# Attention, Fourier mixing and feed-forward in one kernel: the first batch without transfers inside SBUF, and a first feed-forward whose two layers follow one another

## The chip, the cores and the metric

The kernel runs on one core of a Trainium2 chip. A core has five engines with queues of their own: TensorE (PE in the profile, with its weight loads as PEld), VectorE (DVE), ScalarE (ACT), GpSimd (POOL) and SyncE (SP, which here only issues DMAs). Each engine takes its instructions in the order of the program, and semaphores tie the engines together. The metric is the device time of one execution in microseconds (us); the profile is of one execution.

## What is computed

The reference takes q, k and v of 8 batches, 8 heads, 576 positions and 64 columns, and two weight matrices (512 x 2048 and 2048 x 512). Cut to what matters:

```python
scores = scale * np.matmul(q, k.transpose(0, 1, 3, 2))
scores = np.where(block_i >= block_j, scores, -1e9)       # blocks of 64 positions
attn = softmax(scores)                                    # over the last axis
x = np.matmul(attn, v), heads side by side                # (8, 576, 512)
u = x + real(fft(fft(x, axis=1), axis=2))
un = (u - mean(u)) / sqrt(var(u) + 1e-6)                  # over the last axis
out = u + np.maximum(un @ w_ch1, 0) @ w_ch2
```

## The kernel before, in words

**Order of the work.** A planner written into the kernel (`Step`, `Queue`, `issue`, and the loop at L922) decides in which order steps are emitted. Each step has a cost on PE, a chain of costs on other engines, keys it comes after, and a place. There are seven lanes: loads of heads, their preparation, v, the maxima, scores, values, and the transform; besides them a lane of weight steps (`weight_lane`) that fills gaps, and the feed-forward as a filler of PE (`feed_steps`). Steps of batch 1 and later are taken only when the last weight step is emitted (key "w32", L930). PE keeps the order of emission (`mm`, `tp`, L193 to L198); the other engines' order follows from a simulation of the program when it is built.

**Precision.** Numbers of 32 bits are split in a high part that a matmul takes exactly and a rest. For a head, `lead` (L292) writes the high part of q and k into the tile `LEAD` (64 rows of data, below them 8 rows that make the mask, and one row, `KS - 1`, that holds for each query a shift: minus its largest score). `rest` (L304) writes the remainders into the tile `REST`: of q by DVE in its upper 64 rows, of k by POOL in its lower 64 rows. `lead_copies` (L299) fills the other halves of `REST` with the high parts, by two DMAs from SBUF to SBUF, so that one matmul of 128 rows gives both mixed products. There are three buffers of each.

**Attention of a head.** `max_part` (L371) computes scores in the high parts alone and reduces them on DVE to a maximum for each query, in the tile `M` (L388 to L394). `shift` (L398) transposes the five columns of `M` on PE, negates them on ACT (L403, tile `mt`) and sends them by a DMA to the last row of `LEAD` (L405). In batch 0 `quick` (L295) puts these DMAs on ACT's queue, later on SP's. `scores` (L417) then needs two matmuls for each piece of columns: `rest` by `rest` (L430) and `lead` by `lead` (L432), the latter with mask and shift. ACT takes the exponential twice, to fp16 (`ph`, L434) and to fp32 (`p`, L435), and POOL subtracts (`pl`, L436). `values` (L441) multiplies by v, whose parts `VH` and `VL` come from L339 and L340; DVE divides by the sums (L471 to L474), and after every second head SP stores x to DRAM (L479).

**Transform.** `fourier_steps` (L522) loads and gathers the batch, folds it (L549 to L564, tiles `tmp`, `fs`), multiplies by cosines and sines (tiles `zc`, `zs`, `ZT`) and adds to u. `normalized_steps` (L678) normalizes a half of a batch, transposes it (L703) and hands it to `feed_steps` with a running number; number 1 is the first half of batch 0.

**Weights.** They are loaded as 18 blocks (`LANDS`, L811): 14 of two row groups that land in parts of the tile `W` not yet used, four single ones in tiles `u`. `weight_single` (L830) merges the two words of each number on DVE (L836 to L838) and sums squares on ACT (L839); `weight_loads` (L821) then lets SP load ahead, up to `FLIGHT` blocks counted from the one at hand. `weight_scale` (L844) finds a scale, `weight_parts` (L859) makes the two fp16 parts: for w1 on ACT and POOL (L863, L866, L867), for w2 on ACT and DVE (L863, L869).

**Feed-forward.** `first` (L729) computes a column block f of the hidden layer in `h` (twelve matmuls); for every second f ACT and DVE make its two fp16 parts `gh` and `gl` (L749, L750), in tiles with two buffers each. `second` (L752) multiplies them by w2 into `acc`. The order is: first layer of f = 0, 1, then always the first layer of the next two and the second layer of the last two (L785 to L793). In feed number 1 a first-layer step comes after the parts of w1 that it reads, a second-layer step after its part of w2.

Of the kernel before, what the change touches and what calls it, by code (L numbers as in the profile page):

```python
# [22 lines left out]
P = 128  # L23
# [15 lines left out]
FLIGHT = 3  # L39
# [6 lines left out]
KS = KM + 1  # L46
# [25 lines left out]
def _constants():  # L72
# [45 lines left out]
    masks = np.zeros((9, 64 + 2 * S))  # L118
    masks[8, 64 + S:] = 1.0
# [59 lines left out]
def tile_attn_fourier_ffn(  # L179
# [45 lines left out]
    REST = [const.tile([P, 2 * S], F32R, name=f"rest{i}") for i in range(NB)]  # L225
    M = [const.tile([P, 6], F32, name=f"M_{i}") for i in range(2)]
    DEN = [const.tile([P, 5], F32, name=f"DEN_{i}") for i in range(2)]
# [67 lines left out]
    def quick(h):  # L295

        return nc.scalar if h < H else nc.sync

    def lead_copies(h):  # L299
        x0, x1 = REST[h % NB].bitcast(F32), LEAD[h % NB].bitcast(F32)  # L300
        quick(h).dma_start(x0[D:P, 0:S], x1[0:D, 64:64 + S])
        quick(h).dma_start(x0[0:D, S:], x1[0:D, 64 + S:])

    def rest(h, which):  # L304
# [4 lines left out]
        else:  # L309
            nc.gpsimd.tensor_tensor(x0[D:P, S:], raw[:, S:], x1[0:D, 64 + S:], op=ALU.subtract)  # L310
# [38 lines left out]
    def prepare_lane():  # L349
        for h in range(B * H):  # L350
# [4 lines left out]
            yield Step(lambda: lead_copies(h), 0.0, ("A1.0" if h < H else "Q1.2", "L2.2"), (("T", h),), ("TC", h), place=h - 0.9)  # L355
# [15 lines left out]
    def max_part(h, n):  # L371

        m = M[h % 2]
# [13 lines left out]
        if n == 0:  # L387
            nc.vector.tensor_reduce(  # L388
                m[:, 0:6:5], t[:, 0:128].rearrange("p (x y) -> p x y", y=64), axis=AX.X, op=ALU.max
            )  # L390
        j, lo, hi = parts[-1]
        nc.vector.tensor_reduce(m[:, j:j + 1], t[:, at - hi:at], axis=AX.X, op=ALU.max)  # L392
        if n == 3:
            nc.vector.tensor_tensor(m[:, 4:5], m[:, 4:5], m[:, 5:6], op=ALU.max)  # L394
# [3 lines left out]
    def shift(h):  # L398
# [5 lines left out]
        dst = LEAD[h % NB][KM:KS, 0:640].rearrange("r (j p) -> r j p", j=5)  # L404
        quick(h).dma_start(dst.bitcast(F32), mt.bitcast(F32))  # L405
# [11 lines left out]
    def scores(h, n):  # L417
# [9 lines left out]
        for c, lo, width in chunks:  # L427
            first, last = P * c + lo, P * c + lo + width
            keys = S + (P * c if c < 4 else S - P)
            mm(t[:, w:w + width], x0[:, keys:keys + P], x0[:, first:last], start=(w == 0), stop=False, skip_group_check=True)  # L430
# [53 lines left out]
    def score_lane():  # L484
        for h in range(B * H):
            for n, (i, at, chunks) in enumerate(PIECES):
                w = sum(x[2] for x in chunks)
                yield Step(
                    lambda n=n: scores(h, n), w / 1200.0, (_a(w), _a(w), "B", _g(w)),
                    (("X", h), ("TC", h), ("T2", h, 0), ("T2", h, 1)), ("S", h, i) if n else None, True,  # L490
# [3 lines left out]
    def max_lane():  # L494
        for h in range(B * H):
# [5 lines left out]
            yield Step(lambda: shift(h), 0.12, ("A0.26", "B", "A0.5" if h < H else "Q0.6", "L2.2"), (("M", h),), ("X", h), True, place=h - 0.6)  # L501
# [222 lines left out]

# [288 lines left out]
```

## Time and profile before

| what | value |
| --- | --- |
| median of 3 runs | 1315.72 us (1313.14 to 1316.76) |
| the profiled execution's own time | 1315.5 us |
| its span, first to last instruction | 1313.7 us |
| PE busy | 1184.2 us, 90% of the span |
| DVE, ACT, POOL busy | 671.9, 548.5, 530.0 us |
| moved by DMA | 99.10 MB, mean 75 GB/s |

Busy times are sums over the span, so an engine with a small share can still be what a stage waits for. In the rows that follow, a group of instructions has line, engine, operation, output <- input, and count; a row in order of time begins with its start and its length in us, and what stands in brackets is how long the engine was idle before it and what ended that. Names ending in q (ACTq, SPq) are the instructions by which an engine issues DMAs.

### The profile page before, as it was taken

To read this page: it belongs to the slowest core of one execution; us is meant where nothing else is said; L and a number is where in the kernel's file an instruction comes from. 1 tells how busy PE (TensorE), PEld (TensorE's weight loads), DVE (VectorE), ACT (ScalarE), POOL (GpSimd) and SP (SyncE) were. 2 spreads that over 40 slices of the span, in tenths; PEclk is the share of its full clock that TensorE was granted. 3 is DMA by queue.
4 is the path that set the end of the run, shared out by engine and by line. 5 is a ranking of instruction groups with operands and counts; after the bars stand their busy time and mean duration, and the time that the engine had idled before them with its cause. 6 is when DMAs were issued, how large, how long until landed. Compare 5 with 4: busy or idle time off the path is not lost.

```text
span 1313.7 us, 25264 instructions
## 1 busy us (share of the span) xinstructions
PE 1184.2 (90%) x10068; PEld 886.7 (67%) x10068; DVE 671.9 (51%) x1440; ACT 548.5 (42%) x1137; POOL 530.0 (40%) x578
## 2 busy tenths in 40 slices
PE   3464469999898999999999999999899999999998
PEld 2363357777676777677777777777677767767665
DVE  6983776445645564655546544746372432412211
ACT  3569355545354444444545354544543112111110
POOL 4668143444544553455443645436442500300000
PEclk9955679999699999999999999999999999999999
DMA  9756213232223223322242133223211000000000
GB/s 280 230 175 177 93 29 77 84 106 64 61 65 92 76 50 90 93 76 51 80 115 75 44 96 104 73 70 86 79 30 49 30 12 17 22 1 17 16 17 17
DMA packets 55941, 99.10 MB, mean 75 GB/s; under 512 B 7709, under 2 KB 26605, under 8 KB 55696
## 3 DMA queue, kind: packets, MB, share of 16 engines
q1 hardware_dynamic: 52176, 87.56, 23.5%
q0 software_dynamic: 2288, 7.54, 1.9%
q10 hardware_dynamic: 1360, 2.38, 0.6%
q8 instruction: 80, 1.31, 0.4%
q14 instruction: 37, 0.30, 0.1%
HBM read 58.46 MB, written 18.87 MB: 59 GB/s over the span
## 4 chain that ended last, share of the span: by engine, by line
PE 76%; DVE 10%; ACT 4%; DMA 3%; POOL 3%; issue 3%; SPq 0%; ACTq 0%; DVEq 0%; POOLq 0%
PE h L194 27%; PE acc L194 26%; PE ps L194 16%; PE av L194 5%; POOL pl L436 2%; PE ps L197 1%; DVE M L392 1%; DVE W L837 1%; DMA W<-in_moe_w_ch_dram 1%; DVE rest L308 1%; DVE W L838 1%; ACT lead L293 1%; DVE tmp L549 1%; DMA U<-xd,rows 1%; DVE W L836 1%
## 5 line engine op out<-in xcount | busy, mean ns | idle before, releaser
L194 PE MATMUL h<-uh,W 128*128 128x256 f16 x2304 | 434.9, 275 | 0.0
L436 POOL TENSOR_TENSOR pl<-p,ph 128x288 f16<-128x288 f32 (+1 forms) x256 | 257.9, 1017 | 395.8 <-ACT p L435 249.6
L194 PEld LDWEIGHTS <-W 128*128 128x128 f16 x3456 | 325.8, 99 | 64.3 <-issue 4.0
L194 PE MATMUL acc<-W,gh 128*128 128x512 f16 x1152 | 347.2, 383 | 0.0
L194 PE MATMUL h<-ul,W 128*128 128x256 f16 x1152 | 316.2, 274 | 0.0
L194 PE MATMUL acc<-W,gl 128*128 128x512 f16 x576 | 220.1, 382 | 0.4 <-DVE gl L750 0.4
L750 DVE SCALAR_TENSOR_TENSOR gl<-h,gh 128x512 f16<-128x512 f32 x144 | 98.9, 687 | 227.3 <-ACT gh L749 227.2
L194 PE MATMUL ps<-lead 72*128 72x64 f32 (+9 forms) x700 | 196.5, 342 | 12.5 <-ACT lead L293 6.8
L749 ACT ACTIVATE gh<-h 128x512 f16<-128x512 f32 x144 | 85.9, 596 | 268.4 <-PE h L194 267.7
L434 ACT ACTIVATE ph<-ps 128x512 f16<-128x512 f32 (+1 forms) x229 | 116.0, 507 | 121.0 <-PE ps L194 119.7
L194 PEld LDWEIGHTS <-gh 128*128 128x128 f16 x1152 | 101.0, 99 | 87.8 <-issue 8.2
L392 DVE TENSOR_REDUCE M<-ps 128x1 f32<-128x320 f32 (+3 forms) x235 | 120.5, 527 | 47.9 <-PE ps L194 46.7
L194 PE MATMUL av<-VH,pl 128*128 128x65 f16 x960 | 115.9, 200 | 31.7 <-POOL pl L436 31.5
L194 PEld LDWEIGHTS ps<-lead 72*128 72x128 f32 (+1 forms) x700 | 125.6, 201 | 20.8 <-ACT lead L293 6.8
L194 PEld LDWEIGHTS <-ph 128*128 128x128 f16 x1920 | 113.0, 103 | 34.1 <-DVE x L474 8.4
L310 POOL TENSOR_TENSOR rest<-raw,lead 64x576 fp32r<-64x576 f32 x64 | 116.2, 1816 | 23.3 <-ACT lead L293 18.5
L194 PE MATMUL av<-VH,ph 128*128 128x65 f16 x960 | 118.1, 202 | 8.2 <-DVE x L474 7.6
L194 PE MATMUL ps<-rest 128*128 128x64 f32 (+2 forms) x345 | 121.6, 360 | 1.8 <-DVE M L392 1.1
L435 ACT ACTIVATE p<-ps 128x512 f32<-128x512 f32 (+1 forms) x229 | 115.9, 506 | 10.2 <-POOL pl L436 10.1
L194 PE MATMUL av<-VL,ph 128*128 128x64 f16 x960 | 117.3, 200 | 0.0
L194 PEld LDWEIGHTS <-pl 128*128 128x128 f16 x960 | 93.6, 102 | 34.9 <-POOL pl L436 34.8
L308 DVE TENSOR_TENSOR rest<-raw,lead 64x576 fp32r<-64x576 f32 x64 | 60.0, 938 | 88.4 <-ACT lead L293 88.3
(171 smaller groups left out, 1376.7 us busy)
## 6 DMA issues: line engine op xcount, KB each, us to landing
raw<-in_qk_dram SPq DMA_DIRECT2D x64, 288.0 KB
rest<-lead SPq DMA_DIRECT2D x112, 144.0 KB
W<-in_moe_w_ch_dram SPq DMA_DIRECT2D x14, 1024.0 KB
V<-in_v_dram SPq DMA_DIRECT2D x32, 320.0 KB
xd<-x SPq DMA_DIRECT2D x32, 256.0 KB
out_dram<-u SPq DMA_DIRECT2D x32, 256.0 KB
u<-xd SPq DMA_DIRECT2D x8, 512.0 KB
dft<-in_c_dft_dram POOLq DMA_DIRECT2D x1, 2606.0 KB, 11.3
```

The costliest lines, as they stand in the source:

```text
L194: return tc.keep_in_program_order(nc.tensor.matmul(*args, **kw))
L197: return tc.keep_in_program_order(nc.tensor.transpose(*args, **kw))
L293: nc.scalar.copy(LEAD[h % NB][0:D, 64:], raws[h])
L308: nc.vector.tensor_tensor(x0[0:D, 0:S], raw[:, 0:S], x1[0:D, 64:64 + S], op=ALU.subtract)
L310: nc.gpsimd.tensor_tensor(x0[D:P, S:], raw[:, S:], x1[0:D, 64 + S:], op=ALU.subtract)
L392: nc.vector.tensor_reduce(m[:, j:j + 1], t[:, at - hi:at], axis=AX.X, op=ALU.max)
L434: nc.scalar.activation(ph[:, at:at + w], t[:, 0:w], AF.Exp, scale=0.125)
L435: nc.scalar.activation(p32[:, 0:w], t[:, 0:w], AF.Exp, scale=0.125)
L436: nc.gpsimd.tensor_tensor(pl[:, at:at + w], p32[:, 0:w], ph[:, at:at + w], op=ALU.subtract)
L549: nc.vector.tensor_tensor(e[0:r], X[c][0:r], U[c][0:r], op=op)
L749: nc.scalar.activation(gh, t, AF.Relu)
L750: nc.vector.scalar_tensor_tensor(gl, t, 0.0, gh, op0=ALU.max, op1=ALU.subtract)
```

## The change

It has four parts. (1) For the heads of batch 0 (h < H) nothing is copied inside SBUF. `lead_copies` is not called; `scores` makes the mixed products by two matmuls of 64 rows, one with the high part of k and the rest of q, one the other way round, and POOL writes the rest of k into the upper 64 rows. The shift row is made by PE: the maxima are written into a column of a tile of zeros, `MZ`, so that a matmul of 97 columns (`shift_row`) puts them, transposed, at partition 96 of PSUM, from where ACT writes the row of `LEAD` directly. For that the row moves from partition 72 to 96 (`KS = D + 33`), with rows of zeros between; the loaded mask has 33 rows in place of 9. `shift_row` is two steps, of four matmuls and of one. `MZ` lies in the memory of the transform's tiles `zc0` and `zc1` and is cleared at the start. (2) Later heads use the same row, and their DMAs stay on SP. (3) `FLIGHT` is 2 in place of 3. (4) Feed number 1 does its first layer for all 16 blocks and then its second; the tiles `gh` and `gl` from f = 5 on lie in the transform's tiles `zc`, `zs` and `fs`.

```diff
--- before.py
+++ after.py
@@ -36,14 +36,14 @@
 AHEAD = (1.5, 6.0)
 FREE = 0.5
 
-FLIGHT = 3
+FLIGHT = 2
 
 PSHIFT = 5
 
 BANKS = {"ps": 3, "h": 2, "acc": 2}
 
 KM = D + 8
-KS = KM + 1
+KS = D + 33
 
 
 def _a(width):
@@ -115,8 +115,8 @@
         [chunks(csh, csl), chunks(ssh, ssl), stack_c, stack_s, chunks(cdh, cdl), chunks(sdh, sdl), tail], 1
     ).astype(np.float32)
 
-    masks = np.zeros((9, 64 + 2 * S))
-    masks[8, 64 + S:] = 1.0
+    masks = np.zeros((KS - D, 64 + 2 * S))
+    masks[-1, 64 + S:] = 1.0
     for c in range(4):
         masks[c, 64 + 128 * c:128 + 128 * c] = 1.0
         masks[c, 64 + S + 128 * c + 64:64 + S + 128 * c + 128] = NEG
@@ -223,7 +223,22 @@
     NB = 3
     LEAD = [const.tile([KS, 64 + 2 * S], F32R, name=f"lead{i}") for i in range(NB)]
     REST = [const.tile([P, 2 * S], F32R, name=f"rest{i}") for i in range(NB)]
+
     M = [const.tile([P, 6], F32, name=f"M_{i}") for i in range(2)]
+    MZ = [
+        work.tile([P, 2, NCOS], F32R, name=f"zc{i}", bufs=1).bitcast(F32).rearrange("p x n -> p (x n)") for i in range(2)
+    ]
+    for i in range(2):
+        nc.vector.memset(MZ[i], 0.0)
+
+    def maximum(h, j):
+        at = j if h >= H else KS * (j + 1) - 1 if j < 5 else KS * 5 + 1
+        return (M if h >= H else MZ)[h % 2][:, at:at + 1]
+
+    def outer_maxima(h):
+
+        return M[h % 2][:, 0:6:5] if h >= H else MZ[h % 2][:, KS - 1:KS * 5 + 2:KS * 4 + 2]
+
     DEN = [const.tile([P, 5], F32, name=f"DEN_{i}") for i in range(2)]
     VH = [const.tile([P, 5, 2, D + 1], F16, name=f"VH_{i}") for i in range(2)]
     VL = [const.tile([P, 5, 2, D], F16, name=f"VL_{i}") for i in range(2)]
@@ -292,14 +307,10 @@
     def lead(h):
         nc.scalar.copy(LEAD[h % NB][0:D, 64:], raws[h])
 
-    def quick(h):
-
-        return nc.scalar if h < H else nc.sync
-
     def lead_copies(h):
         x0, x1 = REST[h % NB].bitcast(F32), LEAD[h % NB].bitcast(F32)
-        quick(h).dma_start(x0[D:P, 0:S], x1[0:D, 64:64 + S])
-        quick(h).dma_start(x0[0:D, S:], x1[0:D, 64 + S:])
+        nc.sync.dma_start(x0[D:P, 0:S], x1[0:D, 64:64 + S])
+        nc.sync.dma_start(x0[0:D, S:], x1[0:D, 64 + S:])
 
     def rest(h, which):
 
@@ -307,7 +318,8 @@
         if which == 0:
             nc.vector.tensor_tensor(x0[0:D, 0:S], raw[:, 0:S], x1[0:D, 64:64 + S], op=ALU.subtract)
         else:
-            nc.gpsimd.tensor_tensor(x0[D:P, S:], raw[:, S:], x1[0:D, 64 + S:], op=ALU.subtract)
+            at = slice(0, D) if h < H else slice(D, P)
+            nc.gpsimd.tensor_tensor(x0[at, S:], raw[:, S:], x1[0:D, 64 + S:], op=ALU.subtract)
 
     def load_v(g):
         V = vraw[g] = work.tile([P, 5, 2, D], F32, name="V", bufs=1)
@@ -352,7 +364,8 @@
                 lambda: lead(h), 0.0, ("A1.15",), (("L", h),), ("T", h), place=h - 1.0,
                 need=(("S", h - NB, 2),) if h >= NB else (),
             )
-            yield Step(lambda: lead_copies(h), 0.0, ("A1.0" if h < H else "Q1.2", "L2.2"), (("T", h),), ("TC", h), place=h - 0.9)
+            if h >= H:
+                yield Step(lambda: lead_copies(h), 0.0, ("Q1.2", "L2.2"), (("T", h),), ("TC", h), place=h - 0.9)
             yield Step(lambda: rest(h, 0), 0.0, (_d(S),), (("T", h),), ("T2", h, 0), place=h - 0.8)
             yield Step(lambda: rest(h, 1), 0.0, (_g(S),), (("T", h),), ("T2", h, 1), place=h - 0.8)
 
@@ -370,7 +383,6 @@
 
     def max_part(h, n):
 
-        m = M[h % 2]
         x = LEAD[h % NB][0:KM]
         kh = x[:, 64 + S:]
         qh = lambda j: x[:, P * j:P * (j + 1)]
@@ -386,12 +398,12 @@
             at += hi - lo
         if n == 0:
             nc.vector.tensor_reduce(
-                m[:, 0:6:5], t[:, 0:128].rearrange("p (x y) -> p x y", y=64), axis=AX.X, op=ALU.max
+                outer_maxima(h), t[:, 0:128].rearrange("p (x y) -> p x y", y=64), axis=AX.X, op=ALU.max
             )
         j, lo, hi = parts[-1]
-        nc.vector.tensor_reduce(m[:, j:j + 1], t[:, at - hi:at], axis=AX.X, op=ALU.max)
+        nc.vector.tensor_reduce(maximum(h, j), t[:, at - hi:at], axis=AX.X, op=ALU.max)
         if n == 3:
-            nc.vector.tensor_tensor(m[:, 4:5], m[:, 4:5], m[:, 5:6], op=ALU.max)
+            nc.vector.tensor_scalar(maximum(h, 4), maximum(h, 4), maximum(h, 5), None, op0=ALU.max)
 
     MAXPARTS = (((0, 0, 64), (4, 512, 576), (1, 0, 192)), ((2, 0, 320),), ((3, 0, 448),), ((4, 0, 512),))
 
@@ -401,8 +413,23 @@
         tp(t[0:5, 0:P], M[h % 2][:, 0:5], ident)
         mt = work.tile([5, P], F32R, name="mt", bufs=2)
         nc.scalar.activation(mt, t[0:5, 0:P], AF.Copy, bias=float(8.0 * PSHIFT * np.log(2.0)), scale=-1.0)
-        dst = LEAD[h % NB][KM:KS, 0:640].rearrange("r (j p) -> r j p", j=5)
-        quick(h).dma_start(dst.bitcast(F32), mt.bitcast(F32))
+        dst = LEAD[h % NB][KS - 1:KS, 0:640].rearrange("r (j p) -> r j p", j=5)
+        nc.sync.dma_start(dst.bitcast(F32), mt.bitcast(F32))
+
+    def shift_row(h, part):
+
+        t = ps_tile()
+        js = range(4) if part == 0 else range(4, 5)
+        for j in js:
+            at = P * (j - js[0])
+            mm(
+                t[0:KS, at:at + P], MZ[h % 2][:, KS * j:KS * (j + 1)], ident, start=(j == js[0]), stop=(j == js[-1]),
+                skip_group_check=True,
+            )
+        nc.scalar.activation(
+            LEAD[h % NB][KS - 1:KS, P * js[0]:P * (js[-1] + 1)], t[KS - 1:KS, 0:P * len(js)], AF.Copy,
+            bias=float(8.0 * PSHIFT * np.log(2.0)), scale=-1.0,
+        )
 
     probs = {}
 
@@ -427,7 +454,15 @@
         for c, lo, width in chunks:
             first, last = P * c + lo, P * c + lo + width
             keys = S + (P * c if c < 4 else S - P)
-            mm(t[:, w:w + width], x0[:, keys:keys + P], x0[:, first:last], start=(w == 0), stop=False, skip_group_check=True)
+            if h < H:
+                k1, q1 = x1[0:D, 64 + keys:64 + keys + P], x1[0:D, 64 + first:64 + last]
+                mm(t[:, w:w + width], k1, x0[0:D, first:last], start=(w == 0), stop=False, skip_group_check=True)
+                mm(t[:, w:w + width], x0[0:D, keys:keys + P], q1, start=False, stop=False, skip_group_check=True)
+            else:
+                mm(
+                    t[:, w:w + width], x0[:, keys:keys + P], x0[:, first:last], start=(w == 0), stop=False,
+                    skip_group_check=True,
+                )
             keys, w = keys + 64, w + width
             mm(t[:, w - width:w], x1[:, keys:keys + P], x1[:, 64 + first:64 + last], start=False, stop=True, skip_group_check=True)
         p32 = work.tile([P, 512], F32, name="p32", bufs=2)
@@ -486,8 +521,8 @@
             for n, (i, at, chunks) in enumerate(PIECES):
                 w = sum(x[2] for x in chunks)
                 yield Step(
-                    lambda n=n: scores(h, n), w / 1200.0, (_a(w), _a(w), "B", _g(w)),
-                    (("X", h), ("TC", h), ("T2", h, 0), ("T2", h, 1)), ("S", h, i) if n else None, True,
+                    lambda n=n: scores(h, n), w / (800.0 if h < H else 1200.0), (_a(w), _a(w), "B", _g(w)),
+                    (("X", h), ("T2", h, 0), ("T2", h, 1)) + ((("TC", h),) if h >= H else ()), ("S", h, i) if n else None, True,
                     need=(("V", h - 1, 2 * i),) if h else (), place=h,
                 )
 
@@ -498,7 +533,13 @@
                     lambda n=n: max_part(h, n), 0.03 + sum(x[2] - x[1] for x in MAXPARTS[n]) / 2400.0, (f"D{(0.65, 0.49, 0.63, 0.93)[n]}",),
                     (("T", h),), ("M", h) if n == 3 else None, True, place=h - 0.6,
                 )
-            yield Step(lambda: shift(h), 0.12, ("A0.26", "B", "A0.5" if h < H else "Q0.6", "L2.2"), (("M", h),), ("X", h), True, place=h - 0.6)
+            if h < H:
+                yield Step(lambda: shift_row(h, 0), 1.0, (_a(4 * P),), (("M", h),), ("X0", h), True, place=h - 0.6)
+                yield Step(lambda: shift_row(h, 1), 0.3, (_a(P),), (("M", h),), ("X", h), True, place=h - 0.6)
+            else:
+                yield Step(
+                    lambda: shift(h), 0.12, ("A0.26", "B", "Q0.6", "L2.2"), (("M", h),), ("X", h), True, place=h - 0.6
+                )
 
     def value_lane():
         for h in range(B * H):
@@ -722,6 +763,9 @@
     n_norm = 0
     feeds = []
 
+    KEEP = [(f"z{x}{m}", [P, 2, n], 1) for x, n in (("c", NCOS), ("s", NSIN)) for m in range(2)]
+    KEEP += [(f"fs{m}", [P, 2, KCOL], 1) for m in range(2)]
+
     def feed_steps(me, uh, ul, us, stores):
         acc = []
         gs = {}
@@ -742,8 +786,14 @@
                 i += 1
             if f % 2 == 0 or part < NK - 1:
                 return
-            gh = work.tile([P, 4 * P], F16, name="gh", bufs=2)
-            gl = work.tile([P, 4 * P], F16, name="gl", bufs=2)
+            if me == 1 and f > 3:
+
+                name, shape, bufs = KEEP[f // 2 - 2]
+                both = work.tile(shape, F32R, name=name, bufs=bufs).rearrange("p x n -> p (x n)").bitcast(F16)
+                gh, gl = both[:, 0:4 * P], both[:, 4 * P:8 * P]
+            else:
+                gh = work.tile([P, 4 * P], F16, name="gh", bufs=2)
+                gl = work.tile([P, 4 * P], F16, name="gl", bufs=2)
             for x in range(2):
                 gs[f - 1 + x] = (gh[:, 2 * P * x:2 * P * (x + 1)], gl[:, 2 * P * x:2 * P * (x + 1)])
             nc.scalar.activation(gh, t, AF.Relu)
@@ -782,6 +832,11 @@
                     ("F", me) if f == NF - 1 and n == 1 else None,
                 )
 
+        if me == 1:
+            for steps in (first_steps, second_steps):
+                for f in range(NF):
+                    yield from steps(f)
+            return
         yield from first_steps(0)
         yield from first_steps(1)
         for f in range(0, NF, 2):
```

## The prediction

> **What bounds the kernel now.** I read the page's slices first: TensorE (PE) is full for most of the span and thin at its beginning. So I cut the span where the work changes and read busy times by stretch (columns: stretch, its length, then busy us and instructions of PE, PEld, DVE, ACT, POOL, the granted clock, DMA share, GB/s).
>
> ```profile
> 0.00:27.00 27.00, 6.66 (x22) 5.40 (x23) 16.46 (x40) 7.70 (x10) 8.85 (x26) 1.00 0.92 277
> 27.00:62.00 35.00, 16.37 (x117) 13.80 (x116) 34.97 (x47) 20.17 (x43) 22.26 (x12) 1.00 0.79 252
> 62.00:103.00 41.00, 27.96 (x288) 25.02 (x287) 34.42 (x67) 29.26 (x61) 29.81 (x23) 0.67 0.59 190
> 103.00:127.00 24.00, 11.31 (x110) 9.38 (x109) 8.91 (x20) 21.47 (x41) 21.79 (x20) 0.50 0.56 147
> 127.00:180.00 53.00, 24.75 (x157) 20.31 (x157) 36.35 (x87) 21.57 (x49) 20.00 (x26) 0.63 0.25 81
> 180.00:210.00 30.00, 25.81 (x213) 18.79 (x213) 23.50 (x42) 23.19 (x44) 13.29 (x11) 0.86 0.20 52
> 210.00:320.00 110.00, 108.30 (x992) 81.86 (x991) 54.67 (x129) 52.50 (x114) 44.27 (x43) 0.98 0.29 79
> 320.00:360.00 40.00, 33.76 (x244) 25.84 (x243) 26.37 (x60) 15.08 (x31) 22.46 (x31) 0.74 0.27 74
> ```
>
> After 210 PE is nearly full, apart from a dip at 320 to 360. The change touches no work there, so it gains what it brings forward before 210. Batch 0's attention ends at 127; then a chain of latencies (store of x, gather, transform, normalization) runs to 180, where feed-forward begins. In 27 to 62 VectorE (DVE) is the bound: 34.97 of 35 us. In 103 to 127 it is idle and ACT and POOL are 90% busy: heads that came late meet the scaling of w1 (L863, L866, L867).
>
> Why are the heads late? Head 0, on PE, ACT, DVE and POOL in order of time:
>
> ```profile
> 15.01 0.58 PE L194 MATMUL h<-rest 128*128 128x288 f32 x1 [0.53 <-DMA rest<-lead]
> 25.35 0.61 PE L194 MATMUL h<-lead 73*128 73x288 f32 x1 [9.77 <-DMA lead<-mt]
> ...
> 12.74 0.27 ACT L403 ACTIVATE mt<-acc 5x128 fp32r<-5x128 f32 x1 [2.52 <-PE acc L197]
> 19.57 1.27 ACTq L405 DMA_DIRECT2D lead<-mt  x1
> 20.88 0.83 ACT L339 ACTIVATE VH<-V,vacc 128x640 f16<-128x640 f32 x1 [7.88 <-issue]
> ...
> 6.76 0.75 DVE L308 TENSOR_TENSOR rest<-raw,lead 64x576 fp32r<-64x576 f32 x1 [4.55 <-ACT lead L293]
> 10.93 1.34 DVE L394 TENSOR_TENSOR M<-M 128x1 f32<-128x1 f32 x1
> 21.75 0.88 DVE L340 SCALAR_TENSOR_TENSOR VL<-V,vacc,VH 128x640 f16<-128x640 f32 x1 [4.43 <-ACT VH L339]
> ...
> 25.50 8.35 POOL L310 TENSOR_TENSOR rest<-raw,lead 64x576 fp32r<-64x576 f32 x1 [13.24 <-ACT lead L293]
> ```
>
> The maxima are complete at 12.27, the row is ready at 13.0, its DMA is issued only at 19.57, and PE goes on at 25.35. ACT stands behind that issue for 7.88 us, DVE behind ACT for 4.43, POOL has nothing for 13.24. This is what the change takes away.
>
> **The change part by part.** *Transfers of batch 0.* Gone are, for eight heads, two copies and one row, all issued by ACT:
>
> ```profile
> L301 ACTq DMA_DIRECT2D rest<-lead x8: 468/492/561, 7.1 to 92.7; - x8
> L302 ACTq DMA_DIRECT2D rest<-lead x8: 468/608/615, 7.7 to 93.3; - x8
> L405 ACTq DMA_DIRECT2D lead<-mt x8: 728/736/1271, 19.6 to 104.3; - x8
> ...
> 87.20 0.63 ACT L434 ACTIVATE ph<-acc 128x512 f16<-128x512 f32 x1
> ```
>
> That is 8 x (0.49 + 0.61 + 0.74) = 14.7 us of ACT's queue. Added is a 512-wide copy from PSUM per head, like the 0.63 us row, and a 128-wide one in place of L403: 8 x 0.6 = 5 us. ACT is about 10 us lighter. The new copies wait for PE as L403 did, with the same exponentials and weight squares queued behind them.
>
> PE gets dearer. The scores' first matmul becomes two of 64 rows, so the columns of the `rest` matmuls run once more; five fp32 matmuls of 128 columns replace one transpose. The nearest rows:
>
> ```profile
> 26.24 0.57 PE L194 MATMUL ps<-rest 128*128 128x448 f32 x1
> 26.61 0.57 PE L194 MATMUL ps<-lead 73*128 73x448 f32 x1
> ...
> 172.08 1.08 PE h L197 x4
> ...
> 97.01 0.30 PE L194 MATMUL h<-vacc,ones 128*128 128x1 f32 x2
> ```
>
> At half clock 448 columns take 0.37 us from start to start, so the 1600 columns of a head take 1.3. Four transposes of 128 fp32 columns last 1.08, or (1.08 - 0.42) / 3 = 0.22 each, their single duration being 0.42:
>
> ```profile
> L197 PE MATMUL h<-ident,un x8: 421/421/456, 172.1 to 174.5; 128*128 128x128 f32 x8
> ```
>
> One fp32 matmul that is no transpose (L330) left two records, so a shift matmul costs 0.22 to 0.44, the five 1.1 to 2.2. Together 2.4 to 3.5 us per head at half clock, 19 to 28 for eight; PE is idle 65 of the first 127 us, so I put it at nothing on the path and keep the price for a rival. The Trainium skill, FP8 and Floating Point Precision, section TensorE Precision Notes, says that true fp32 takes four passes through the array. By that, at the cold 1.2 GHz of TensorE: Matmul & The Clock Gate, the five would be an estimate of 5 x 128 x 4 / 1.2 GHz = 2.1 us; the two records here fit the dearer end, and the sum would stay.
>
> From the maxima to a head's scores the new path is 2 to 3.5 us (those matmuls, 0.6 and 0.3 of ACT); for head 0 it was 13.1. What passes to the end of batch 0? At least DVE's gap, 4.4 us, because DVE bounds the next stretch. At most all idle time of DVE after its start at 6.8: 127 - 94.8 busy - 6.8 = 25 us. Between them I look at the pitch of heads once the weights let go:
>
> ```profile
> 78.35 0.21 DVE L471 TENSOR_SCALAR DEN<-av,vacc 128x5 f32<-128x5 f32 x1
> 102.35 0.22 DVE L471 TENSOR_SCALAR DEN<-av,vacc 128x5 f32<-128x5 f32 x1 [0.82 <-PE av L194]
> 125.62 0.23 DVE L471 TENSOR_SCALAR DEN<-av,vacc 128x5 f32<-128x5 f32 x1 [2.00 <-PE av L194]
> ```
>
> Three heads in 24.0 us: 8.0 each. If heads stand one further when the weights end, 4.4 + 8.0 = 12.4 us go. I take **10**, near the 9.77 that PE waited for that first row.
>
> *Two weight blocks ahead in place of three* (the loop asks up to its own number plus FLIGHT).
>
> ```profile
> L836 DVE TENSOR_SCALAR W<-W x14: 674/688/1893, 12.3 to 84.3; 128x1024 int32<-128x1024 int32 x14
> ...
> 78.39 0.37 SPq L826 DMA_DIRECT2D W<-in_moe_w_ch_dram  x1
> 129.84 9.13 SPq L826 DMA_DIRECT2D u<-in_moe_w_ch_dram  x4
> ```
>
> A block is merged every 5.5 us, and the last of the 14 came 5.9 us after its issue. A block asked for one step later on SP may come late by up to that pitch; on the other side the third raw head shares the DMA with fewer weights at the start. From block 4 on, the landing places already hold a load back until an older block is merged. I take 0; DVE has head work to do meanwhile, and without that cover it costs what DVE then waits. The memsets and the larger mask lie in DVE's first idle us.
>
> *First layer as a whole in feed-forward 1.* PE runs its first layer from 180.7, waits, and can start the second only at 195.4:
>
> ```profile
> 180.73 0.42 PE L194 MATMUL h<-ul,W 128*128 128x256 f16 x1
> 192.70 0.20 PE L194 MATMUL av<-VH,pl 128*128 128x65 f16 x1 [1.48 <-POOL pl L436]
> 195.38 1.08 PE L194 MATMUL acc<-W,gh 128*128 128x512 f16 x2
> ```
>
> In 180 to 210 PE is idle 4.2 us, and a clock of 0.86 takes 30 x 0.14 = 4.2 more. More first layer brings at most both, 8.4. At least 0: feeds that end sooner leave the dip at 320 to 360 (6.2 us idle) longer, until batch 1's transform, which they don't hasten. I take **3**. The kept tiles reuse transform buffers; feed 1 ended long before batch 1's first fold:
>
> ```profile
> 253.70 0.71 DVE L761 SCALAR_TENSOR_TENSOR u<-acc,inv_w,u 128x512 f32<-128x512 f32 x1
> 289.58 1.75 DVE L549 TENSOR_TENSOR tmp<-X,U 33x512 f32<-33x512 f32 x1 [3.59 <-DMA U<-xd,rows]
> ```
>
> 36 us to spare, so 0; beyond them each us would delay that fold.
>
> Sum: span 1313.7 - 10 - 3 = 1300.7, plus 1.8 around it (1315.5 - 1313.7): **1302.5 us**. The profiled 1315.5 and the median 1315.72 are the same within what can be told.
>
> **The rivals.**
> 1. *Heads stay where DVE's order puts them.* DVE takes head steps and weight merges in a fixed order, and was full to 62; then only the gap of 4.4 and part of the 3 come: 1315.5 - 6.5 = 1309. For it: 34.97 of 35. Against: 21.7 idle us of DVE in 62 to 127, which are order, not load.
> 2. *Batch 0 becomes gapless.* ACT 10 us lighter, no row in a DMA queue: most of the 25 goes, 1315.5 - 25 - 3 = 1288. Against: the w1 scaling on POOL and ACT must still fit, and their 90% at 103 to 127 leave little.
> 3. *Gained and given back.* The dip at 320 to 360 grows, or weight blocks come late by as much as the heads gain: 1315. For it: the transform of batch 0 waits for the four late weight blocks too, which stand behind the store of x on SP (129.84).
> 4. *Slower: PE becomes the bound of batch 0 at half clock.* Place: 62 to 103, PE 27.96 of 41, at 8.0 us a head five heads. 5 x 3.5 = 17.5 more makes 45.5, 4.5 over the stretch, with nothing gained: 1320. It decides from 13 / 5 = 2.6 us a head on. Against it: work that starts sooner fills 0 to 62, where PE idles 39 us, and a busier PE may get the full clock. For that row: 15 values matmuls took 0.82 us at 58.74 and 0.47 at 97.61.
>
> ```profile
> 58.74 0.82 PE av L194 x15
> ...
> 97.61 0.20 PE L194 MATMUL av<-VH,ph 128*128 128x65 f16 x1
> 98.08 0.48 PE L194 MATMUL acc<-lead 72*128 72x512 f32 x1
> ```
>
> The page's clock for the first 62 us reads 1.00, but the 0.82 is half speed. The Trainium skill, TensorE: Matmul & The Clock Gate, section What's actually happening, has the clock go to full after about 3.4 us of sustained work; by that the five matmuls and extra scores would halve in price and rival 4 would fall away; this trace shows both speeds, not the rule.
>
> **How the numbers follow.** The forecast (1296 to 1308) has 0.55, rival 1 0.13, rival 2 0.12, rival 3 0.08, rival 4 0.12. About 0.3%, 4 us, can be told from no change: faster 0.55 + 0.13 + 0.12 = 0.80, same 0.08, slower 0.12. The range 1288 to 1318 takes in all but rival 4 and the far end of rival 2.
>
> **What would show it.** Right: no `lead<-mt` or `rest<-lead` on ACT's queue; head 0's second score matmul near 16 in place of 25.35; the eighth L471 near 115 in place of 125.62; first `h<-uh,W` near 170; `acc` only after all first-layer steps, with no gap of 5 us behind the first ones. Wrong: DVE waiting for `W` loads before 90 (rival 3), PE over 90% of 62 to 103 without a full clock (rival 4), or batch 0 ending earlier and the dip near 320 to 360 longer by the same.

## The result, and the profile after

| | median of 4 (range) | profiled execution | its span | mean clock |
|---|---|---|---|---|
| before | 1315.28 us (1313.14 to 1316.76) | 1315.5 us | 1313.7 us | 0.951 |
| after | 1328.14 us (1325.2 to 1334.71) | 1325.2 us | 1323.0 us | 0.937 |

The change makes the kernel slower by 1.1%: the ratio is 1.0106, 95% interval 1.0061 to 1.0151. The forecast was 1302.5 us, 1288 to 1318.

The stretches of the changed kernel (columns as in the prediction: stretch, length, busy us and instructions of PE, PEld, DVE, ACT, POOL, granted clock, DMA share, GB/s):

```profile
0.00:27.00 27.00, 17.86 (x83) 13.33 (x83) 19.34 (x42) 11.90 (x20) 12.21 (x30) 1.00 0.95 251
27.00:62.00 35.00, 28.07 (x153) 20.81 (x151) 31.31 (x44) 19.93 (x38) 22.98 (x11) 0.59 0.76 247
62.00:103.00 41.00, 39.27 (x268) 30.06 (x268) 32.34 (x58) 27.68 (x56) 22.06 (x18) 0.60 0.49 158
103.00:127.00 24.00, 22.52 (x145) 16.18 (x141) 9.95 (x28) 15.75 (x32) 11.70 (x11) 0.61 0.44 130
127.00:180.00 53.00, 19.51 (x104) 14.62 (x105) 31.49 (x72) 23.85 (x50) 21.39 (x28) 0.63 0.24 81
180.00:210.00 30.00, 29.87 (x275) 25.72 (x273) 19.13 (x42) 21.27 (x40) 12.33 (x12) 0.94 0.12 32
...
300.00:380.00 80.00, 64.04 (x503) 52.42 (x502) 50.57 (x120) 39.98 (x89) 50.66 (x59) 0.72 0.32 88
```

Compare the first number of each row with before. In 62 to 103 PE is busy 39.27 of 41 us, where it was 27.96, and 22.52 of 24 behind that, where it was 11.31: PE has become the bound of batch 0's attention. The second place is 300 to 380, of which the prediction looked at the middle only. The same stretch of the kernel before:

```profile
300.00:380.00 80.00, 72.71 (x613) 55.78 (x611) 45.78 (x99) 36.98 (x78) 40.70 (x47) 0.87 0.25 66
```

Busy time times clock makes 63.3 us at full speed before and 46.1 after: 17.2 us of PE are lost there. At 180 to 210 the same product is 28.1 against 22.2, so 5.9 come back. The rest from 127 to 440 gives -3.3 (127 to 180), +3.4 (280 to 300) and +2.3 (400 to 440), so 8.9 us are lost in all, near the 9.3 us by which the spans differ. This is a count by rounded clocks, and a rough one.

Head 0 does what the change says. On PE and ACT:

```profile
16.05 0.61 PE L194 MATMUL h<-rest,lead 64*128 64x288 f32 x1
16.45 0.44 PE L194 MATMUL h<-lead,rest 64*128 64x288 f32 x1
16.82 0.61 PE L194 MATMUL h<-lead 97*128 97x288 f32 x1
...
12.66 0.59 ACT L429 ACTIVATE lead<-acc 1x512 fp32r<-1x512 f32 x1
13.90 0.83 ACT L351 ACTIVATE VH<-V,vacc 128x640 f16<-128x640 f32 x1 [0.65 <-DVE vacc L349]
```

The row is written at 12.66, ACT waits 0.65 us in place of 7.88, and the third score matmul starts at 16.82, where before the second one started at 25.35. But look where the heads end. L506 (L471 before) is a head's last step on DVE; each row gives count, min/median/max ns, and the first and last start, for batch 0 and then batch 1. Before:

```profile
L471 DVE TENSOR_SCALAR DEN<-av,vacc x8: 208/224/226, 43.7 to 125.6; 128x5 f32<-128x5 f32 x8
...
L471 DVE TENSOR_SCALAR DEN<-av,vacc x8: 208/215/224, 177.2 to 276.8; 128x5 f32<-128x5 f32 x8
```

After:

```profile
L506 DVE TENSOR_SCALAR DEN<-av,vacc x8: 205/224/226, 37.7 to 132.2; 128x5 f32<-128x5 f32 x8
...
L506 DVE TENSOR_SCALAR DEN<-av,vacc x8: 204/224/225, 199.1 to 293.1; 128x5 f32<-128x5 f32 x8
```

The first head ends 6.0 us earlier and the eighth 6.6 later: (132.2 - 37.7) / 7 = 13.5 us a head, where it was 11.7. Batch 1 begins 21.9 us later and ends 16.3 later, and its transform, and with it the work that fills 300 to 380, comes that much later (its first fold at 305.42, 289.58 before). Feed-forward 1, the second part of the change, begins at 178.54 (180.50 before) and ends at 241.84 (253.70 before):

```profile
178.54 0.42 PE L194 MATMUL h<-uh,W 128*128 128x256 f16 x1
...
241.84 0.73 DVE L811 SCALAR_TENSOR_TENSOR u<-acc,inv_w,u 128x512 f32<-128x512 f32 x1
```

What a head costs on PE is read from start to start. From the scores of one head of batch 0 in the changed kernel:

```profile
63.30 0.60 PE L194 MATMUL ps<-rest,lead 64*128 64x288 f32 x1
63.70 0.44 PE L194 MATMUL ps<-lead,rest 64*128 64x288 f32 x1
64.07 0.61 PE L194 MATMUL ps<-lead 97*128 97x288 f32 x1
64.61 0.61 PE L194 MATMUL h<-rest,lead 64*128 64x288 f32 x1
...
68.43 0.26 PE L194 MATMUL av<-VH,ph 128*128 128x65 f16 x1
...
69.77 0.63 PE L194 MATMUL acc<-rest,lead 64*128 64x320 f32 x1
...
72.16 1.91 PE L194 MATMUL acc<-ident,zc 128*97 128x128 f32 x8
73.86 0.64 PE L194 MATMUL ps<-ident,zc 128*97 128x128 f32 x2
```

The first two digits of `64*128` are the rows of the weights. Four chunks take 63.30 to 68.43, two take 69.77 to 72.16: 7.52 us for a head's scores. A piece of 288 columns takes 0.40, 0.37 and 0.54, 1.31 us, though three passes of 288 columns are 0.71 by the 0.37 for 448 of before. The shift matmuls left ten records, 1.70 / 8 = 0.21 us each: 2.1 us a head.

### The profile page after: what moved, and what is told of

Its sections match the earlier page's. It is cut to its first block, busy times and chain, and to the rows that moved or that the text cites. A ratio compares the mean times of both kernels' runs of the same rounds, so it can differ in the third digit from the quotient of the medians.

```text
span 1323.0 us, 25472 instructions
## 1 busy us (share of the span) xinstructions
PE 1232.8 (93%) x10188; PEld 919.5 (70%) x10188; DVE 669.2 (51%) x1442; ACT 557.9 (42%) x1145; POOL 531.2 (40%) x578
## 3 DMA queue, kind: packets, MB, share of 16 engines
q8 instruction: 80, 1.31, 0.4%
## 4 chain that ended last, share of the span: by engine, by line
PE 79%; DVE 10%; DMA 3%; issue 3%; POOL 2%; ACT 1%; SPq 0%; DVEq 0%; POOLq 0%; ACTq 0%
PE h L194 27%; PE acc L194 27%; PE ps L194 17%; PE av L194 6%; DVE M L404 1%; PE ps L197 1%; DMA xd<-x 1%; DVE tmp L590 1%; POOL pl L471 1%; DMA W<-in_moe_w_ch_dram 1%; DVE W L892 1%; DVE W L891 1%; ACT lead L308 1%; POOL u L579 1%; DVE VL L352 1%
## 5 line engine op out<-in xcount | busy, mean ns | idle before, releaser
L471 POOL TENSOR_TENSOR pl<-p,ph 128x288 f16<-128x288 f32 (+1 forms) x256 | 261.3, 1029 | 361.4 <-ACT p L470 212.1
L194 PE MATMUL acc<-W,gh 128*128 128x512 f16 x1104 | 329.7, 380 | 0.0
L194 PE MATMUL ps<-lead 97*128 97x64 f32 (+5 forms) x717 | 209.5, 351 | 9.8 <-ACT lead L308 7.2
L800 DVE SCALAR_TENSOR_TENSOR gl<-h,gh 128x512 f16<-128x512 f32 x138 | 94.9, 687 | 238.9 <-ACT gh L799 238.7
L194 PE MATMUL acc<-W,gl 128*128 128x512 f16 x552 | 209.2, 379 | 1.5 <-DVE gl L800 1.5
L799 ACT ACTIVATE gh<-h 128x512 f16<-128x512 f32 x138 | 82.2, 595 | 281.2 <-PE h L194 280.7
L469 ACT ACTIVATE ph<-ps 128x512 f16<-128x512 f32 (+1 forms) x237 | 119.8, 505 | 132.3 <-PE ps L194 126.7
L194 PEld LDWEIGHTS ps<-lead 97*128 97x128 f32 (+1 forms) x717 | 131.2, 204 | 24.0 <-ACT lead L308 7.2
L404 DVE TENSOR_REDUCE M<-ps 128x1 f32<-128x512 f32 (+1 forms) x221 | 114.6, 531 | 45.1 <-PE ps L194 43.5
L194 PE MATMUL ps<-rest 128*128 128x288 f32 x336 | 120.2, 364 | 5.9 <-DVE M L404 2.7
L319 DVE TENSOR_TENSOR rest<-raw,lead 64x576 fp32r<-64x576 f32 x64 | 55.4, 866 | 111.2 <-ACT lead L308 94.5
```

The source lines that it names most:

```text
L194: return tc.keep_in_program_order(nc.tensor.matmul(*args, **kw))
L319: nc.vector.tensor_tensor(x0[0:D, 0:S], raw[:, 0:S], x1[0:D, 64:64 + S], op=ALU.subtract)
L404: nc.vector.tensor_reduce(maximum(h, j), t[:, at - hi:at], axis=AX.X, op=ALU.max)
L469: nc.scalar.activation(ph[:, at:at + w], t[:, 0:w], AF.Exp, scale=0.125)
L471: nc.gpsimd.tensor_tensor(pl[:, at:at + w], p32[:, 0:w], ph[:, at:at + w], op=ALU.subtract)
L799: nc.scalar.activation(gh, t, AF.Relu)
```

## The experiments

Theory when they began: PE's dearer scores bind batch 0 (rival 4), and the late batch 1 is a second loss. Rivals: the shift matmuls, the two weight blocks ahead, or the new order of feed-forward 1. Each kernel's time, a median in us, stands with its ratio to the kernel before, run beside it (medians 1313.25 to 1315.41), and the 95% interval of that ratio.

**One part at a time.** a1 is the changed kernel without its other two parts:

```
-FLIGHT = 2
+FLIGHT = 3
-        if me == 1:
-            for steps in (first_steps, second_steps):
...
```

> Part 1 alone (no transfers in batch 0; three blocks ahead, feed-forward 1 in its old order). If the dearer PE work of batch 0 is the cause, batch 0 still ends near 132 (eighth L506 or its like) and the time is 1322 to 1328. If the order of feed-forward 1 is the cause, batch 0 may end late all the same, but batch 1's heads follow as soon as before, feed 3 starts near 360 and the time is 1312 to 1320.

a2 is the kernel before with that block and its kept tiles put in, a3 the kernel before with `FLIGHT = 2`.

> The kernel before with feed-forward 1 in the new order alone. If that order is the cause: batch 0 ends at 126 as before, PE is full in 180 to 210, batch 1's heads end some 10 us later, the dip around 300 to 380 is deeper, time 1320 to 1328. If PE's work in batch 0 is the cause: 1310 to 1316, a gain of up to 5.

> The kernel before with two weight blocks ahead in place of three, nothing else. Either theory: 1313 to 1319. If late weight blocks are the cause, DVE waits for W loads before 90, batch 0 ends at 130 or later and the time is 1320 or more.

Measured: a1 1330.61 (1.0131, 1.0115 to 1.0148), a2 1310.9 (0.9982, 0.9971 to 0.9993), a3 1314.41 (1.0002, 0.9993 to 1.0012). The loss is in the transfers; the new order of feed-forward 1 alone gains about 2.4 us and the block less in flight costs nothing. a1 lies above the 1322 to 1328 that its text gave to PE's work. In its profile batch 0 ends at 136.3, at a granted clock of 0.50 in 62 to 103, and in that of a6 below, with the same work of PE, at 136.6 and 0.50; the changed kernel's 132.2 came at 0.60. So a single end of batch 0 is known to no better than some 4 us.

**The transfers in two halves.** a7 keeps the copies and two score matmuls of before, the copies on ACT's queue, and lets PE make the row; a8 does the opposite, three score matmuls and no copies, the row by transpose and DMA on ACT's queue.

```
a7:
...
+            mm(t[:, w:w + width], x0[:, keys:keys + P], x0[:, first:last], start=(w == 0), stop=False, skip_group_check=True)
...
+        quick = nc.scalar if h < H else nc.sync
...
a8:
...
+        (nc.scalar if h < H else nc.sync).dma_start(dst.bitcast(F32), mt.bitcast(F32))
```

> Only the shift row is made by PE; the two copies stay DMAs and a piece has its two matmuls as before (feed-forward 1 in the new order, two blocks ahead). If the third score matmul with its 64 rows is the cause: batch 0 ends at 126 or earlier, time 1305 to 1314. If the shift matmuls are: batch 0 at 130 or later, 1320 or more. If the order is: over 1320 with batch 0 earlier.

> Only the copies are gone and a piece has three matmuls; the shift row goes by transpose and DMA as before (feed-forward 1 in the new order, two blocks ahead). If the third score matmul is the cause: batch 0 near 130, time 1320 to 1332. If the shift matmuls are: 1308 to 1316.

Measured: a7 1315.91 (1.0008, 0.9998 to 1.0018), a8 1332.33 (1.0127, 1.011 to 1.0144). The third score matmul carries the loss. a7 doesn't gain either: it lies above the 1305 to 1314 expected and 0.3% above a2, which has the same feed-forward 1, although its batch 0 ends at 122.4. a4 takes work off PE at another place: the five shift matmuls become transposes.

```
-            mm(
-                t[0:KS, at:at + P], MZ[h % 2][:, KS * j:KS * (j + 1)], ident, start=(j == js[0]), stop=(j == js[-1]),
...
+            tp(t[0:KS, at:at + P], MZ[h % 2][:, KS * j:KS * (j + 1)], ident)
```

> The changed kernel with the five shift matmuls of a head made as PE transposes (one record each in place of two), so about 1.1 us of PE less per head at half clock, 8 to 9 us over batch 0. If PE bounds batch 0: its attention ends near 124 in place of 132 and the time falls by 5 to 8, to 1317 to 1323. If the order of feed-forward 1 is the cause: batch 0 ends earlier or not, the time stays at 1324 to 1330.

Measured: 1329.79 (1.0113, 1.0096 to 1.013). Batch 0 ended at 126.6, 5.6 us earlier (in an execution of 1333.69), and the time did not move. Its text gave that outcome to the order of feed-forward 1, but a2 shows that this order alone costs nothing. The store of x was issued at 129.38 (133.18 in the changed kernel) and the fold began at 147.59 (147.80). SP's queue and DVE's in a4:

```profile
127.31 0.52 SPq L313 DMA_DIRECT2D rest<-lead  x1
128.79 0.49 SPq L305 DMA_DIRECT2D raw<-in_qk_dram  x1
129.38 0.54 SPq L511 DMA_DIRECT2D xd<-x  x1
...
141.85 2.97 DVE L890 SCALAR_TENSOR_TENSOR W<-u,W 128x512 int32<-128x512 int32 x1
```

The store stands behind the copies and the raw load of a head of batch 1. Of the 5.6 us 3.8 are left at the store and 2.5 at the first merge of a late weight block on DVE (140.66 against 143.15). The other 2.3 go in the merge step shown last, which takes 2.97 us in place of 0.69, and the fold comes behind these merges. That SP's order holds the store was not tried by itself, nor is it shown why that one merge is long.

**Why the third matmul is dear.** a5 gives all three the same 97 rows (rows 64 to 127 of `rest` cleared once, so the sum stays); a13 gives the first two 65 rows; a10 keeps 64 but puts the 64-row matmuls of a piece first.

```
a5:
...
-                k1, q1 = x1[0:D, 64 + keys:64 + keys + P], x1[0:D, 64 + first:64 + last]
+                k1, q1 = x1[0:KS, 64 + keys:64 + keys + P], x1[0:KS, 64 + first:64 + last]
...
a13: the same with 0:D + 1
a10:
...
+        for first, last, keys, a, b in parts:
+            mm(t[:, a:b], x1[:, keys + 64:keys + 64 + P], x1[:, 64 + first:64 + last], start=False, stop=(b == w), skip_group_check=True)
```

> The changed kernel with all three score matmuls of a piece on 97 rows (rows 64 to 96 of the rests are zero, cleared once by ACT), so that no weight load changes between 64 and 97 rows. If the change of tile height is what makes PE slow in batch 0, a 288-column piece takes 3 x 0.24 us at half clock in place of 0.41 + 0.37 + 0.53, a head 3 to 4 us less, the eighth DEN comes at 105 to 118 in place of 132. If PE in batch 0 is then the cause of the loss, the time is 1310 to 1318. If the order of the steps behind batch 0 is the cause (batch 1's heads behind feed-forward 1), batch 0 ends earlier and the time stays over 1320.

> The changed kernel, the two rest matmuls of the scores on 65 rows in place of 64 (row 64 of the rest tile is cleared once, so the sum stays the same); the last one stays at 97. Theory A: PE handles matmuls of at most 64 rows in another way than those of more, and the passage from one to the other is what costs, so that 65 behaves like 97: 0.24 us from start to start at 288 columns and half clock, about 3.1 us a head of scores, 1320 (1316 to 1324). Rival B: each change of the number of rows costs, whatever the numbers: 0.37 to 0.53 as in the changed kernel, 7.7 us a head, 1328 (1325 to 1332).

> The changed kernel with the 64-row matmuls of a score piece first and its 97-row ones behind them: the two pieces of two chunks then change height twice in place of four times, 8 changes a head in place of 12. Theory A (the passage costs): in these two pieces the second, third and fourth 64-row matmul follow each other at 0.24 us for 288 columns (0.37 for 448), and a head becomes 1.5 us cheaper, a third of 4.6: 1325.5 (1322 to 1329). Rival C: a 64-row matmul is dear by itself, because its weights are not loaded beside the one ahead: the spacing stays 0.16 us over the columns' own time between 64-row ones, and only the 97-row ones gain, 0.3 us a head: 1328 (1325 to 1331).

Measured: a5 1320.09 (1.0034, 1.0014 to 1.0053), a13 1317.14 (1.002, 1.0007 to 1.0033), a10 1319.04 (1.0047, 1.0029 to 1.0065). In a5 batch 0 ends at 122.2, not at the 105 to 118 expected, and its time lies 2 us above the range given for PE as the only cause. A head's scores in a13, at half clock as above:

```profile
63.36 0.59 PE L194 MATMUL ps<-rest,lead 65*128 65x288 f32 x1
63.75 0.44 PE L194 MATMUL ps<-lead,rest 65*128 65x288 f32 x1
63.99 0.44 PE L194 MATMUL ps<-lead 97*128 97x288 f32 x1
64.23 0.44 PE L194 MATMUL h<-rest,lead 65*128 65x288 f32 x1
...
66.57 0.26 PE L194 MATMUL av<-VH,ph 128*128 128x65 f16 x1
...
67.84 0.61 PE L194 MATMUL acc<-rest,lead 65*128 65x320 f32 x1
...
69.37 0.84 PE L194 MATMUL acc<-ident,zc 128*97 128x128 f32 x3
```

One row more in the weights, and the spacing falls from 0.37 and 0.54 to 0.24 and 0.24. The head takes 3.21 + 1.53 = 4.74 us in place of 7.52. A mere change of the number of rows costs nothing (65 beside 97), so rival B falls; what costs is the passage between 64 rows and more. In a10, a piece of 320 and 192 columns:

```profile
84.84 0.63 PE L194 MATMUL ps<-rest,lead 64*128 64x320 f32 x1
85.27 0.47 PE L194 MATMUL ps<-lead,rest 64*128 64x320 f32 x1
85.54 0.36 PE L194 MATMUL ps<-rest,lead 64*128 64x192 f32 x1
85.70 0.41 PE L194 MATMUL ps<-lead,rest 64*128 64x192 f32 x1
86.04 0.79 PE L194 MATMUL ps<-lead 97*128 97x320 f32 x2
86.63 1.91 PE L194 MATMUL h<-ident,zc 128*97 128x128 f32 x8
```

Between 64-row matmuls 320 columns take 0.27, as from 68.25 to 68.52 in a13, so they aren't dear by themselves, and rival C falls. The piece takes 1.79 us, 2.39 in the changed kernel and 1.53 in a13: two passages in place of four, and none. Twelve passages a head make 7.52 - 4.74 = 2.78 us, 0.2 us each; this piece gives 0.1 to 0.3. The Trainium skill, TensorEngine Tiling (Array Packing), section Key Properties, says that a change of tiling mode drains TensorE, and its Available Configurations list 64 rows as a mode of its own; the boundary between 64 and 65 rows fits that, if these matmuls run in that mode, which no run here shows. What the traces do show is the weight load (PEld). Here are the loads for the 97-row matmul of the first piece and for the one behind it, first in the changed kernel, where those matmuls start at 64.07 and 64.61, then in a13, where they start at 63.99 and 64.23:

```profile
64.07 0.29 PEld L194 LDWEIGHTS ps<-lead 97*128 97x128 f32 x1 [0.27 <-issue]
64.61 0.28 PEld L194 LDWEIGHTS h<-rest,lead 64*128 64x128 f32 x1 [0.25 <-issue]
```

```profile
63.75 0.33 PEld L194 LDWEIGHTS ps<-lead 97*128 97x128 f32 x1
63.99 0.33 PEld L194 LDWEIGHTS h<-rest,lead 65*128 65x128 f32 x1
```

In a13 a load starts 0.24 us ahead of its matmul, beside the matmul in front. At a passage it starts together with its own matmul, so it is no longer hidden.

a10's gain of 9 us is more than the 3 expected: its batch 0 ends at 124.7, where a13's, without any passage, ends at 122.0, so the last passages seem to bind little. Its granted clock in 62 to 103 was 0.75, where the changed kernel had 0.60; how much of the gain is the clock wasn't separated.

**The order behind batch 0.** In the changed kernel PE is busy 19.51 of 53 us at 127 to 180, yet batch 1's first scores come at 186.8, behind the first steps of feed-forward 1; before, they stood at 162.1. a6 lets two heads of batch 1 pass ahead of the merge of w2, which they otherwise wait for in the planner's order; a9 is a5 with it, a11 is a2 with it, a12 is a7 with it.

```
-            if x is not None and may(x) and (i == len(lanes) - 1 or x.place < H or "w32" in done)
+            if x is not None and may(x) and (i == len(lanes) - 1 or x.place < H + 2 or "w32" in done)
```

> The changed kernel with the planner's gate moved by two heads: heads 8 and 9 need not wait for the last weight step. If the order is the cause, those heads run in PE's idle time between 133 and 180, batch 1 ends near 277 in place of 293 and the time is 1310 to 1320. If PE in batch 0 is the cause, the time stays at 1324 to 1332.

> The changed kernel with both mends: all three score matmuls on 97 rows (alone worth 8.0 us, 1320.1 beside 1328.1) and the first two heads of batch 1 let in ahead of the merge of w2 (alone worth 7.5 us, 1320.6). Theory: two causes, one inside batch 0's attention and one in the order behind it, that add up: 1328.1 - 8.0 - 7.5 = 1312.6, range 1309 to 1316, with batch 0's last values step near 122 and batch 1's heads begun before 165. Rival: both mends fill the same idle time between 133 and 187, so that the second brings little once the first is there: 1317 to 1321.

> The kernel before with the new order of feed-forward 1 and the two first heads of batch 1 let in ahead of the merge of w2. Theory: the order behind batch 0 cost the changed kernel 7.5 us because its heads came late; in the kernel before the heads of batch 1 already stood in PE's idle time at 160 to 165, so this brings 0 to 2 us over the new order alone (1310.9): 1309 to 1312. Rival: letting them in is worth as much anywhere: 1303 to 1305.

> The row by PE with the copies still made by DMA and two score matmuls (alone 1315.9, batch 0 ending at 122.4 but batch 1 beginning late at 185.0), and the first two heads of batch 1 let in ahead of the merge of w2. Theory: the end of batch 0's attention doesn't set the time; what counts is that batch 1's first heads fill PE's idle time behind it: 1311 (1308 to 1314), where the new feed order alone and the changed kernel with both mends stand (1310.9 and 1310.8). Rival: each us of batch 0's end passes through to the end of the kernel: 1310.9 less the 2.3 us by which batch 0 ends earlier than there, or 1308 and below.

Measured: a6 1320.62 (1.0048, 1.0033 to 1.0064), a9 1310.77 (0.9983, 0.9966 to 1.0), a11 1313.84 (1.0, 0.9989 to 1.0011), a12 1307.99 (0.9944, 0.9926 to 0.9962). a6 (the profiled execution took 1325.55):

```profile
127.00:180.00 53.00, 31.02 (x237) 25.45 (x236) 39.33 (x71) 32.42 (x70) 30.68 (x26) 0.58 0.39 120
...
300.00:380.00 80.00, 73.12 (x608) 56.60 (x607) 46.76 (x111) 39.64 (x87) 42.39 (x49) 0.84 0.25 66
```

The idle time at 127 to 180 fills, and 300 to 380 is back at 61.4 us of PE at full speed, near the 63.3 of before. a6 lies just above its 1310 to 1320. a6 and a5 give 7.5 and 8.0 us and together 17.4 (by the ratios 0.6%, 0.7% and 1.2%): two causes that add up, and the rival of a9 falls. In the kernel before, whose heads already came at 162, letting them in gains nothing (a11, at 1313.8 a little above the 1309 to 1312 expected), so the rival there falls. a12's theory was wrong and its rival right: 1308.0, with an interval that lies below a9's. Its batch 0 ends at 121.5 and a9's at 124.1, which fits an earlier end that reaches the end of the kernel; the two differ in their score matmuls too, so that isn't shown by itself.

The late batch 1 isn't just the delay of batch 0 handed on. The heads of a13, in batch 0 and in batch 1:

```profile
L509 DVE TENSOR_SCALAR DEN<-av,vacc x8: 204/218/225, 37.3 to 122.0; 128x5 f32<-128x5 f32 x8
```

```profile
L509 DVE TENSOR_SCALAR DEN<-av,vacc x8: 203/224/225, 189.8 to 283.8; 128x5 f32<-128x5 f32 x8
```

Batch 0 ends 3.6 us earlier than in the kernel before, and batch 1 still begins 12.6 us later. The changed kernel also raised the planner's costs of the score steps, but a7 has the old ones and its batch 1 begins at 185.0, against 176.4 in a2. So those costs aren't needed for it; which new step moves the order was not tried.

**What is left of the gain.** a14 has 65 rows, transposes and two heads let in; a15 three heads.

> The changed kernel with all three mends of PE's work and order: 65 rows in the two rest matmuls, the row of maxima by transposes, two heads of batch 1 let in. Theory: with PE relieved, DVE's order of head steps and weight merges holds batch 0's heads (DVE was busy 34.98 of 35 us with 65 rows), so that 1.2 us a head less of PE brings nothing: batch 0 ends at 121 to 124 and the time is 1309 to 1312. Rival: PE at half clock still holds them (39.75 of 41 us busy with 65 rows): batch 0 ends at 115 to 119, 1304 to 1308.

> The same with three heads of batch 1 let in. Theory: two heads already leave feed-forward 1 at 188 to 190, 10 us behind where it began without them, and DVE has 42 of 53 us at 127 to 180; a third head delays feed-forward 1 further and gives back what it fills: 1309 to 1315. Rival: PE still idles 30 us at 127 to 180, so a third head is free: 1303 to 1307.

Measured: a14 1309.85 (0.9958, 0.9941 to 0.9976), a15 1304.62 (0.9917, 0.9889 to 0.9946). a14 in batch 0:

```profile
27.00:62.00 35.00, 22.66 (x141) 19.27 (x142) 35.00 (x48) 21.87 (x44) 22.90 (x11) 1.00 0.66 221
62.00:103.00 41.00, 36.63 (x271) 32.92 (x271) 37.07 (x62) 25.14 (x51) 27.21 (x18) 1.00 0.55 188
```

and its heads, then those of a15 in batch 1, with a15's dip:

```profile
L506 DVE TENSOR_SCALAR DEN<-av,vacc x8: 204/212/224, 38.4 to 123.7; 128x5 f32<-128x5 f32 x8
```

```profile
L506 DVE TENSOR_SCALAR DEN<-av,vacc x8: 206/210/224, 144.4 to 260.8; 128x5 f32<-128x5 f32 x8
```

```profile
300.00:380.00 80.00, 75.76 (x730) 59.20 (x729) 43.99 (x103) 41.38 (x86) 46.20 (x52) 1.00 0.27 74
```

The clock column reads 1.00 in a14's two rows, but its 288 columns take 0.24 us there too (matmuls at 63.58, 63.82 and 64.06), which is half speed. With PE relieved, DVE is busy 35.00 of 35 us, and batch 0 ends at 123.7, as a14's theory had it, not at 115 to 119. In 62 to 103 DVE with 37.07 us and PE with 36.63 are alike, so there it stays open which of them binds. For a15 its rival was right: the third head ends batch 1 at 260.8, where a14's ends at 269.5, the dip at 300 to 380 nearly closes, and the time is 0.8% below the kernel before, 1.8% below the changed one. This version beats both kernels.

## Why the prediction was wrong

The forecast was wrong in sign; rival 4 had the mechanism inside batch 0, at a chance of 0.12, and its sign came as named: PE over 90% of 62 to 103 without a full clock. Its 1320 has no late batch 1 in it, which a6 puts at 7.5 us.

- *What the change removes* was right: the rows at head 0 show the 7.88 us of ACT gone and the scores started 8.5 us earlier (25.35 to 16.82).
- *The step that failed: "PE is idle 65 of the first 127 us, so I put it at nothing on the path".* The price was 2.4 to 3.5 us a head. The runs show the third pass at 1.4 to 1.6 (4.74 in a13 less the 3.1 to 3.4 of a head's two passes in a2, at the same half speed; 1.3 was put), 2.1 for the shift matmuls (the dear end of 1.1 to 2.2) and 2.8 for the passages between 64 and 97 rows, which no row of before could show: 6.3 to 6.5. Eight heads make some 50 us, and idle time of 65 that is spread between dependent steps can't take that in: PE is busy 39.27 of 41. Rival 4 set the turning point at 2.6 us a head, and 6.3 is far beyond it. With the passages gone (a13) batch 0 ends 10.2 us earlier and 11.0 us of time go.
- *The sentence against rival 4*, that a busier PE may get the full clock, failed too. At 39.27 of 41 us busy the granted clock was 0.60, and at 39.26 in a1 and a6 it was 0.50. The Trainium skill, TensorE: Matmul & The Clock Gate, section What's actually happening, has the clock rise after about 3.4 us of sustained work; by busy time alone that is not borne out here, and whether the short gaps between head steps are what kept it down was not tried.
- *"12.4 us go", from DVE's gap and one pitch of 8.0,* failed beside it. Even with PE's cost mended batch 0 ends at 122 to 124 (a13, a14), 2 to 4 us earlier than before and not 10: DVE had been full to 62 before and is full there again (35.00 of 35 in a14), which speaks for rival 1; behind 62 it is not shown.
- *The end of batch 0 was taken to pass to the end one for one.* Here batch 0 ends 6.6 us late and batch 1 begins 21.9 late, since the planner placed batch 1's heads behind the first steps of feed-forward 1; 12.6 of it stand in a13 without any delay of batch 0. I read the dip at 320 to 360 as given, and rival 3 had it grow through feeds that end sooner; it grew through a batch 1 that came later (a6: 7.5 us).
- *Feed-forward 1* was right: taken at 3, measured 2.4 alone (a2), where PE is busy 27.26 of 30 us at 180 to 210 at a clock of 1.00 (25.81 at 0.86 before). *Two blocks in flight* at 0 was right (a3).

The account: a13 takes 11.0 us off the changed kernel's 1328.1, transposes and two heads of batch 1 let in 7.3 more (a14), a third head 5.2 more (a15). That ends at 1304.6, near the forecast, but by steps that the change doesn't make; that it comes near is luck.

## What to carry to other kernels

Before a matmul is split into shorter ones, look at whether their row counts lie on both sides of the step between 64 and 65: each passage cost 0.2 us here at half clock, and one cleared row more removed it. Idle time of an engine takes in added work only where that work's inputs and the order of instructions let it fall there, so set the added cost against the stretch's pitch of heads, not against the sum of idle time. And look at the order that a planner makes of new steps: with batch 0 ending 3.6 us earlier than before (a13), batch 1 still began 12.6 us later.

## What the runs showed of the hardware

At half clock, two matmuls of 64 rows and one of 97 in turn took 0.40, 0.37 and 0.54 us from start to start at 288 columns; with 65 rows in place of 64 they took 0.24 each behind a first of 0.39. A weight load started 0.24 us ahead of its matmul in a13, but together with it at a passage between 64 and 97 rows. A 128-column fp32 matmul that isn't a transpose left two records and took 0.43 us at half clock. PE, busy 96% of a stretch of 41 us, was granted 0.60 of its clock in the changed kernel and 0.50 in a1 and a6.
